# Fourth pair's values cast head by head on two engines, and a new hand-kept order for the first half, in an attention and MLP kernel

## The chip, the cores and the metric

The kernel runs on one core of one Trainium2 chip. The metric is the device time of one execution in microseconds. Seven executions of the kernel before were measured: 233.19 to 238.86 us, with a median of 233.5 us. One further execution was recorded by the hardware profiler; it took 235.44 us.

In the profile the engines have short names. PE is TensorE's matmuls and PEld its weight loads, DVE is VectorE, ACT is ScalarE, POOL is GpSimd, and SP is SyncE, which here only issues DMA transfers.

## What is computed

The inputs are queries, keys and values of shape (4 batches, 8 heads, 768 positions, 64). Heads 0, 2 and 6 are "retrieval" heads, with full causal attention. The other five are "streaming" heads: a query sees the first four positions (the sinks) and the 64 latest ones. The attention output, as 3072 tokens of 512 channels, goes through a two-layer MLP with a PReLU between the layers.

```python
scores = scale * np.matmul(q, k.transpose(0, 1, 3, 2))
stream_keep = causal & (is_sink | in_win)
scores = np.where(mask, scores, -1e9)
a = softmax(scores)
x = np.matmul(a, v)                      # to (3072, 512)
h = x @ w_in                             # 512 -> 2048
g = np.maximum(h, 0.0) + alpha * np.minimum(h, 0.0)
out = g @ w_out                          # 2048 -> 512
```

## The kernel before, in words

The work of attention is cut into 16 "pairs" of heads, numbered n = 0 to 15: four pairs for each batch, with heads (2, 6), (1, 5), (0, 4) and (3, 7) in turn. Pair 3 is the fourth pair of batch 0, heads 3 and 7, both streaming. The MLP is cut into eight token blocks t = 0 to 7, two for each batch, of 512 and 256 tokens. Block 0 can begin only when all four pairs of batch 0 are done.

Each piece of work is an "item" with a short name, and the string ORDER (line 14) lists all items. The items are emitted in exactly that order. Each engine runs its own instructions in the order in which they were emitted, so ORDER alone decides what stands behind what on each of the five engines and on each DMA queue. The names that matter here:

- Lq, Lk, Lv n: loads of queries, keys and values of a pair (`load_q`, `load_k`, `load_rows`, lines 204 to 249). They are issued by SyncE and share one hardware DMA queue, in order. A retrieval head's values are one transfer; a streaming head's are two, the second a tail of 24 rows.
- Cq, Ck, Cv n: casts from float32 to bfloat16. The engine is picked by the strings CQ, CK and CV (lines 301 to 303). `cast_v` (line 346) casts both heads of a pair in one instruction, on GpSimd for n below 6, and then calls `sinks` (line 306), which on GpSimd copies the four sink rows of each streaming head into the other six slots.
- Tq, Tk n: transposes of queries and keys on TensorE (`to_array`, line 355), and tq, tk n: the copies of the result out of PSUM.
- S n.h.m: scores on TensorE; s n.h.m: the exponential on ScalarE; m n.h.m: the mask on VectorE from pair 4 on.
- A n.h: the product with the values (line 554), a n.h: the division by the sum on VectorE, X n and x n: the transpose of the result into the MLP's input and its copy.
- P t.f: the first MLP layer for block t and column group f, with p (relu of the negative part on ScalarE) and g (PReLU on VectorE); O t.s: the second layer, with o (copy and store).
- wi0 to wi7 and wo0 to wo3: loads of w_in and w_out, issued by GpSimd on its own software DMA queue, with a cast on the way. wi0 and wi1 serve column groups 0 to 3, wi2 and wi3 groups 4 to 7, wi4 and wi5 groups 8 to 11, wi6 and wi7 groups 12 to 15.
- id, nms, nmr, kz, qz, vz, kfz, warm and others: constants, zero fills and idle matmuls that warm TensorE.

PSUM has eight banks. An item takes the bank that was given back longest ago in ORDER (`take`, line 145), so it can wait for the reader of an older item.

Scores of pairs 4 and later are collected (`one_score`, `emit_burst`, lines 409 to 430) until an item comes up that can't stand beside them. If both heads of the collection have at least 576 columns, the matmuls of the two heads are interleaved on the two halves of TensorE's rows (line 428); if not, they run one after the other (line 421).

Of the kernel before, what the change touches and what calls it, by code (L numbers as in the profile page):

```python
# [11 lines left out]


ORDER = """
Lq0.0 kz3 id zero Lk0 warm0 Ck0.1 qz0 Lk2 La Ck2.0 Lq0.1 vz3 nmr Cq0.0 Cq0.1 vz1 kz0 Lq1 Tq0.0 warm1 Lq2 kz2 Ck0.0
Ck2.1 qz Tk0.0 sz1 sz2 vz0 tq0.0 Cq1 Lk1 warm2 tk0.0 Tk0.1 Lv0 Ck1.0 Cq2 vo S0.0.0 s0.0.0 kz1 tk0.1 Ck1.1 S0.0.2
m6.0.2 Cv0 Tq0.1 m14.0.2 s0.0.2 Lk3 vz2 Tk2 S0.0.1 Lv1 tq0.1 Lq3 Tq1 s0.0.1 tq1 nms Lq5 Ck3.0 S0.1.1 tk2.1 Ck3.1
S0.1.2 Tk1 sz0 s0.1.1 tk2.0 Tq2 S0.1.0 A0.0 Cv1 tk1.0 s0.1.2 S1.0.0 s0.1.0 A0.1 S1.0.1 tq2 s1.0.0 s1.0.1 Lv2 Tk3 wi1
S2.1.1 wi0 so s2.1.1 tk1.1 wi2 S2.1.0 Lk4 a0.0 S1.1.1 s1.1.1 a0.1 X0 Cq3 A1.0 Cv2 Lv3 a1.0 Ck4.1 Lk5 s2.1.0 Cq5 S2.0.2
wi3 Lq4 s2.0.2 S1.1.0 s1.1.0 ro Lk6 Tq3 x0 tq3 S2.0.0 wi6 A1.1 S2.0.1 s2.0.0 wi7 A2.1 tk3.0 s2.0.1 a1.1 Ck4.0 nz1 Cv3  # L20
tk3.1 S3.0.0 S3.0.1 wi5 s3.0.1 s3.0.0 A2.0 a2.1 Tq5 Ck5.0 a2.0 Tk4 S3.1.1 kfz2 Lq6 s3.1.1 wi4 X1 x1 tq5 S3.1.0 X2
s3.1.0 idf x2 A3.0 tk4.0 tk4.1 Lk7 a3.0 P0.2.0 A3.1 P0.1.0 Al P0.1.1 P0.3.0 P0.2.1 a3.1 X3 Ck5.1 P0.3.1 x3 al Lv7 Lv4
P0.0.0 P1.0 P0.2.2 p0.2 P1.4 P0.1.2 p1.4 Cq4 P1.6 P0.3.2 g0.2 P0.0.1 Tk5 p0.1 p0.3 g1.4 g0.1 p1.6 tk5.0 g1.6 kfz3
P0.0.2 p0.0 g0.3 wo0 g0.0 P0.5.0 P1.2 tk5.1 P0.6 p0.6 p1.0 Tq4 P0.13 P0.5.1 P0.4.0 p1.2 g0.6 nz0 p0.13 P0.4.1 wo1 tq4
g1.0 P0.14 g1.2 P0.5.2 g0.13 P1.8 Ck6.1 p0.5 P0.10 Cq6 p1.8 p0.14 P0.4.2 g0.5 Lk8 p0.4 Tq6 Ck6.0 kfz0 tq6 P0.9 Lq7
P0.11 wo3 g1.8 p0.9 g0.14 kfz1 mr p0.10 wo2 g0.4 g0.9 S4.1.3 S4.0.0 S5.0.0 g0.10 S4.1.4 s4.1.3 P0.7 P0.8 s4.0.0 P1.14
p0.11 s4.1.4 p0.8 s5.0.0 Lv5 Cv4 p1.14 S4.1.2 S4.0.4 g0.11 s4.1.2 g0.8 ms P0.15 S4.1.1 s4.0.4 S5.1.2 p0.15 S5.0.2
S4.0.5 g1.14 s5.1.2 P0.12 g0.15 O0.0.0 p0.7 p0.12 P1.10 s4.1.1 s4.0.5 s5.0.2 g0.7 m4.0.5 m5.1.2 Lq8 Cv5 P1.12 S5.1.0
S4.0.3 S4.1.0 S4.0.1 g0.12 s4.0.3 O0.3.0 one m5.0.0 m4.0.0 O0.1.0 m4.1.4 Ck7.1 O0.0.1 O0.0.2 ns s5.1.0 p1.10 s4.1.0
S4.0.2 s4.0.1 m4.0.4 g1.10 m4.0.1 S5.1.1 S4.1.5 m4.0.3 S5.0.1 s5.1.1 m4.1.1 Lk9 s4.1.5 O0.1.1 O0.0.3 Ck7.0 s5.0.1  # L30
m4.1.3 Tk6 m5.1.1 s4.0.2 p1.12 o0.0 Cv7 Ck8 Tk7 A4.0 Cq7 m4.1.5 g1.12 Lv6 m5.1.0 tk6.1 O0.3.1 m5.0.1 Tq7 O0.3.2 m4.0.2
Lq9 tk6.0 tk7.0 Cq8 S6.0.1 S6.0.0 m5.0.2 tq7 A5.1 nr Dk8.1 a5.1 O0.1.2 a4.0 A5.0 O0.1.3 s6.0.1 tk7.1 m4.1.0 o0.1
S6.1.0 S6.1.2 S6.0.2 S6.0.4 a5.0 s6.1.2 Dq8 O0.3.3 m6.1.2 S7.1.2 s6.0.4 s6.0.0 s6.1.0 Dk8.0 O0.2.0 s6.0.2 S7.1.0 o0.3
S6.0.3 S6.0.5 S7.1.1 S6.1.1 Ck9 s7.1.0 O0.2.1 s7.1.2 O0.2.2 Cv6 m6.0.0 s7.1.1 X5 m7.1.0 A4.1 s6.1.1 S8.1.1 x5 s6.0.5
S7.0.2 s6.0.3 m6.0.5 S8.1.5 m6.0.4 S7.0.0 S8.1.4 S7.0.1 m6.0.1 m6.1.1 Dk9.0 m7.1.1 s7.0.1 m6.0.3 s7.0.0 Lv9 O0.2.3
A6.0 Cq9 m7.1.2 s8.1.1 s8.1.5 O1.1.0 a6.0 a4.1 s8.1.4 Dq9 O1.1.1 s7.0.2 m6.1.0 m7.0.0 A7.1 S8.0.0 S8.1.2 S8.1.0 S8.0.1
A6.1 s8.0.0 m7.0.1 m7.0.2 m8.1.1 O1.1.2 s8.0.1 Dk9.1 a6.1 X4 A7.0 a7.0 s8.1.0 X6 a7.1 O1.0.0 O1.0.1 O1.1.3 x6 Lv8 X7
S8.0.3 S9.0.1 Lq10 s8.1.2 Lq11 s9.0.1 Cv9 near1 S9.1.1 x7 O1.0.2 m8.1.0 o0.2 s8.0.3 O1.0.3 S9.1.2 S8.1.3 m8.1.4 S8.0.4
S9.0.2 o1.1 S9.1.0 m8.1.5 S9.0.0 s9.1.1 s8.1.3 s8.0.4 P2.6 Cv8 p2.6 Lk11 o1.0 m8.1.3 Lk10 P2.5 p2.5 P2.14 s9.1.2 P3.0
s9.1.0 s9.0.2 p2.14 P2.3 P2.7 Lq12 g2.6 Lq13 m9.1.0 p2.3 g2.5 s9.0.0 near0 m10.0.2 near2 A8.1 p3.0 g2.14 g2.3 g3.0  # L40
Cq11 p2.7 m9.1.1 m8.0.4 P2.0 p2.0 g2.7 P2.8 Lk12 g2.0 P2.2 p2.8 m9.1.2 S8.0.5 P2.13 p2.2 A9.1 Lk13 m8.0.1 g2.2 s8.0.5
m9.0.0 P3.14 P2.15 p2.13 g2.8 Ck11 P3.8 p2.15 P2.9 a8.1 g2.15 P3.4 P2.1 a9.1 P3.10 Ck10 p3.4 Dk10.0 g2.13 P2.11 p2.1
p3.10 g3.4 S8.0.2 P2.4 s8.0.2 p2.4 g2.1 P2.10 Cq10 Dk10.1 g3.10 p2.9 Dq10 m8.0.5 m8.0.0 P2.12 m8.0.3 P3.6 g2.9 Dk11.1
g2.4 p2.10 A8.0 O2.0.0 g2.10 O2.0.1 p2.11 p3.8 g2.11 Ck12 S10.0.1 S10.0.4 s10.0.1 g3.8 p3.14 O2.0.2 s10.0.4 Dk11.0
O2.1.0 Dq11 p2.12 a8.0 g3.14 S10.1.1 S10.0.0 p3.6 g2.12 m10.0.4 S10.1.0 S10.0.5 s10.1.0 s10.1.1 O2.1.1 Lv11 Cq12
O2.0.3 g3.6 S10.0.3 S11.0.0 m10.1.0 s10.0.5 s10.0.0 S11.1.2 S11.1.0 m9.0.2 S10.1.2 S10.0.2 s10.0.3 Cq13 O2.1.2 m10.0.0
s10.1.2 Lv10 Ck13 m9.0.1 m10.1.2 s11.1.2 m11.1.2 s11.1.0 Dk12.0 P3.2 s10.0.2 p3.2 A9.0 s11.0.0 O2.2.0 Dq12 S11.0.2
S11.1.1 m10.0.5 O2.1.3 S11.0.1 m10.0.3 Cv11 m11.0.0 m10.1.1 Dk13.1 m11.1.0 X8 m10.0.1 s11.1.1 Cv10 P3.12 p3.12 m11.1.1
a9.0 s11.0.1 O2.2.1 g3.2 A10.1 Dk13.0 o2.1 Dk12.1 g3.12 a10.1 Dq13 A10.0 A11.1 O2.2.2 m11.0.1 X9 o2.0 O2.3.0 O2.2.3
S12.1.5 S12.0.4 S12.0.2 a10.0 s11.0.2 S12.1.2 m11.0.2 a11.1 S12.0.1 s12.1.5 A11.0 Lq14 a11.0 X11 O2.3.1 O3.1.0 s12.0.4  # L50
s12.0.2 m12.0.4 X10 S13.0.1 O3.1.1 s12.1.2 Lk15 s12.0.1 S12.0.3 S13.0.2 S13.1.2 s13.0.1 S13.1.1 o2.2 S12.0.0 S12.1.0
s12.1.0 s12.0.0 Lk14 s12.0.3 s13.1.2 O2.3.2 Lv12 O2.3.3 m12.0.3 o2.3 O3.0.0 s13.1.1 s13.0.2 O3.1.2 S12.0.5 S13.1.0
S13.0.0 S12.1.4 P4.0 m12.0.1 P4.1 m13.1.2 Cq14 s13.1.0 s13.0.0 m12.1.0 P4.11 m12.0.0 p4.0 s12.0.5 P4.12 m13.1.0 P4.3
p4.1 g4.0 P4.4 m13.0.1 s12.1.4 p4.12 g4.1 Lq15 P5.6 p4.11 m12.0.5 p4.3 g4.11 O3.0.1 m13.1.1 g4.12 Ck15 g4.3 p4.4 P4.15
P4.13 P4.9 p4.13 Lv13 P5.2 p4.15 Ck14 Dq14 m12.0.2 Cv12 g4.4 g4.13 Dk15.1 P4.10 Cq15 g4.15 p5.6 g5.6 p4.10 P4.6 Cv13
Dk14.0 p4.6 g4.10 g4.6 A12.0 p5.2 O3.0.2 A13.1 O3.0.3 g5.2 a13.1 O3.1.3 P4.7 o3.0 S12.1.1 S14.0.3 P4.14 o3.1 P4.2
Dk14.1 p4.7 p4.9 Dq15 s12.1.1 a12.0 g4.7 g4.9 S15.1.2 S14.0.2 p4.14 S14.0.4 S15.1.1 S14.1.0 s14.0.3 m12.1.4 m12.1.1
p4.2 s14.0.2 P5.12 g4.14 m14.0.3 s14.1.0 P4.5 p5.12 g4.2 P4.8 s15.1.2 m13.0.2 O4.3.0 m13.0.0 Lv15 Dk15.0 s14.0.4 p4.5
S14.0.5 S15.1.0 S14.0.1 s15.1.1 S14.1.2 g5.12 g4.5 m15.1.1 p4.8 S12.1.3 g4.8 S14.0.0 s12.1.3 O4.3.1 A13.0 m12.1.3
s14.0.0 P5.14 Lv14 Cv15 S15.0.2 s14.0.5 s14.1.2 p5.14 S15.0.0 a13.0 m14.1.2 O4.3.2 S15.0.1 S14.1.1 m12.1.5 m15.1.2  # L60
s15.1.0 m14.0.5 Cv14 m15.1.0 s15.0.2 s15.0.0 A12.1 P5.8 A15.1 s14.0.1 m14.1.0 s14.1.1 P5.0 m14.0.1 m14.1.1 A14.1
m14.0.4 s15.0.1 a12.1 m14.0.0 O4.1.0 g5.14 a14.1 X13 A14.0 m15.0.0 P5.4 p5.8 m15.0.1 X12 m15.0.2 a15.1 A15.0 p5.0
a15.0 p5.4 O4.1.1 g5.8 O4.0.0 a14.0 m4.1.2 O4.2.0 g5.4 X15 P5.10 O4.1.2 O4.0.1 O4.2.1 m8.0.2 x15 X14 O4.0.2 P6.8 P6.6
O4.0.3 p5.10 g5.0 P6.1 O4.3.3 O4.2.2 g5.10 P6.7 p6.8 o4.0 p6.7 p6.6 P7.6 g6.7 g6.8 O4.2.3 P6.10 O4.1.3 P6.3 p6.10 o4.3
g6.10 P7.4 o4.2 O5.1.0 O5.1.1 P7.0 p6.1 g6.6 P6.2 g6.1 p6.3 O5.0.0 g6.3 o4.1 P6.13 p6.13 P7.14 g6.13 O5.0.1 p6.2 p7.0
P6.0 g6.2 O5.1.2 P6.5 g7.0 P6.11 p6.0 g6.0 O5.0.2 p6.11 O5.1.3 p7.4 p6.5 g6.11 P7.10 p7.14 m8.1.2 o5.1 g6.5 m12.1.2
P6.9 P6.4 g7.4 p6.9 g6.9 p6.4 O5.0.3 g7.14 P7.2 O6.1.0 P6.15 g6.4 p7.2 P7.12 p6.15 O6.1.1 O6.1.2 g7.2 o5.0 O6.0.0
g6.15 P6.14 P6.12 O6.0.1 p6.14 O7.0.0 O6.0.2 g6.14 p7.6 p7.12 p6.12 g6.12 g7.6 O6.3.0 O6.2.0 O6.2.1 O6.0.3 P7.8 O6.2.2
O6.1.3 g7.12 O6.3.1 p7.8 o6.1 p7.10 O6.3.2 O6.3.3 g7.8 O7.0.1 o6.3 g7.10 o6.0 L0 O6.2.3 O7.0.2 o6.2 O7.0.3 L1 l0 L2
o7.0 l1 l2  # L70
""".split()


@with_exitstack
def kernel(
    ctx: ExitStack,
    tc: tile.TileContext,
    q: bass.AP,
    k: bass.AP,
    v: bass.AP,  # L80
    is_retrieval: bass.AP,
# [7 lines left out]
    nc = tc.nc  # L89
    B, H, S, D = q.shape  # L90
# [9 lines left out]
    NSINK = 4  # L100
# [96 lines left out]
    def heads(n):  # L197
        return PAIRS[n % 4]
# [104 lines left out]
    CV = "PPPPPPVVVVVVVVVV"  # L303
    natq, natk, held = {}, {}, {}

    def sinks(n, rows):

        for hh, h in enumerate(heads(n) if n < LAY else ()):
            if not RETR[h]:
                vh = rows[0:NSINK, hh, :, 0:D].bitcast(fp32)  # L310
                nc.gpsimd.tensor_copy(vh[:, 1:7, :], vh[:, 0:1, :].to_broadcast([NSINK, 6, D // 2]))

    def part_of(buf, hh):
        return buf.rearrange("p a b d -> p (a b d)")[:, 6 * D * hh:6 * D * (hh + 1)]
# [27 lines left out]
        nt = 6 if RETR[heads(n)[hh]] else 7  # L342
        nc.sync.dma_start(kTs[n % NK][hh][:, 0:128 * nt].rearrange("p (i r) -> p i r", r=128),
                          natk[n][:, 896 * hh:896 * hh + 128 * nt], transpose=True)

    def cast_v(n):
        vv = vb[n % NV]
# [416 lines left out]
            item(f"Cq{n}", cast_q, n)  # L764
        item(f"Lk{n}", load_k, n)
        item(f"Lv{n}", load_v, n)
        item(f"Cv{n}", cast_v, n)
        if n < CROSS:
            for hh in range(2):
                item(f"Ck{n}.{hh}", cast_k, n, hh)  # L770
# [87 lines left out]
```

## Time and profile before

| what | value |
|---|---|
| median of seven runs | 233.5 us (233.19 to 238.86) |
| the profiled execution | 235.44 us |
| its span, first to last instruction | 233.7 us |
| TensorE busy | 221.6 us, 95% of the span |
| VectorE, ScalarE, GpSimd busy | 153.4, 138.9, 48.3 us |
| moved by DMA | 36.63 MB, 157 GB/s in the mean |
| granted TensorE clock | 1.00 |
| chain that ended last, by engine | PE 81%, DVE 8%, DMA 4% |

The page gives busy time by engine, a row of 40 slices of the span for each engine (each digit is tenths of a slice, 9 is 90% or more), the chain of work that ended last, and groups of instructions by line. Further views give busy time in chosen stretches (windows), the instructions of one engine in order of time (timeline), and who waited for whom. In a timeline a line has the start, the duration, the engine, the line of the program, the operation with its tiles, and in brackets the idle time ahead of it with what ended it. A busy TensorE is not TensorE at its peak, since the ends of matmuls are modelled. The idle time of an engine that is not the bound costs nothing.

### The profile page before, as it was taken

The page shows a single profiled execution, that of the slowest core. Times are in us where ns is not written, and L with a number is a line of the kernel's source. Part 1 is how long each engine was busy: PE and PEld are TensorE (multiplying, and loading weights), DVE is VectorE, ACT ScalarE, POOL GpSimd, SP SyncE. Part 2 cuts the span into 40 slices and gives each one's busy share as a digit, 9 for nine tenths or more (in the row PEclk, how much of TensorE's full clock was granted, in tenths as well). Part 3 has the DMA queues.
Part 4 walks back from the last instruction along what each step waited for, and adds up shares of the span by engine and source line. Part 5 has one row for each costly group of instructions (what it writes and reads, how often), then busy time and mean ns, then how long its engine had stood idle before and what let it go on. Part 6 is the DMA issues. An engine that isn't in the chain of part 4 may idle for free.

```text
span 233.7 us, 5202 instructions
## 1 busy us (share of the span) xinstructions
PE 221.6 (95%) x1970; PEld 136.5 (58%) x1998; DVE 153.4 (66%) x393; ACT 138.9 (59%) x280; POOL 48.3 (21%) x97
## 2 busy tenths in 40 slices
PE   6989769999999999999999999999999999999994
PEld 5778747555465665566466545655864555554553
DVE  4696646898796855998998267979990245545110
ACT  5578546998699539837764874498522333623231
POOL 3778768001294004000001000010000020000000
PEclk9999999999999999999999999999999999999999
DMA  5989999999999899948999999895310130110033
GB/s 187 307 231 207 229 240 248 206 195 194 240 196 206 170 206 254 247 86 158 194 152 143 259 241 188 158 175 97 72 34 0 45 137 1 45 46 1 0 135 136
DMA packets 92449, 36.63 MB, mean 157 GB/s; under 512 B 79472, under 2 KB 90632, under 8 KB 92424
## 3 DMA queue, kind: packets, MB, share of 16 engines
q1 hardware_dynamic: 86168, 26.97, 56.6%
q0 software_dynamic: 5792, 8.93, 18.4%
q10 hardware_dynamic: 464, 0.40, 0.6%
q8 instruction: 15, 0.25, 0.4%
q14 instruction: 10, 0.08, 0.1%
HBM read 27.55 MB, written 6.29 MB: 145 GB/s over the span
## 4 chain that ended last, share of the span: by engine, by line
PE 81%; DVE 8%; DMA 4%; issue 2%; SPq 1%; POOL 1%; ACT 1%; POOLq 0%; ACTq 0%; DVEq 0%
PE P L619 33%; PE P L599 33%; PE P L554 6%; DMA vf<-in_v_dram 4%; PE P L428 3%; DVE g L611 2%; PE P L421 2%; PE P L702 2%; PE P L638 2%; DVE kT L390 1%; DVE kT L386 1%; DVE xn L565 1%; PE P L579 1%; PE P L361 1%; DVE eR L477 1%
## 5 line engine op out<-in xcount | busy, mean ns | idle before, releaser
L611 DVE SCALAR_TENSOR_TENSOR g<-neg,oma,P 128x512 bf16<-128x512 f32 (+1 forms) x128 | 72.9, 609 | 38.5 <-ACT neg L604 37.3
L599 PE MATMUL P<-xT,w_in_b 128*128 128x256 bf16 (+1 forms) x503 | 89.3, 325 | 0.4
L604 ACT ACTIVATE neg<-P 128x512 f32<-128x512 f32 x96 | 54.8, 605 | 54.0 <-PE P L599 46.5
L619 PE MATMUL P<-w_out_b,g 128*128 128x512 bf16 x349 | 84.7, 379 | 1.4 <-issue 0.5
L599 PEld LDWEIGHTS <-w_in_b 128*128 128x128 bf16 x512 | 48.9, 98 | 32.2 <-issue 0.2
L619 PEld LDWEIGHTS <-g 128*128 128x128 bf16 x368 | 34.1, 98 | 36.2 <-issue 1.6
L467 ACT ACTIVATE eR<-P 128x448 bf16<-128x448 f32 (+6 forms) x63 | 36.0, 620 | 12.8 <-PE P L460 3.5
L629 POOL DMA_DIRECT2D out_dram<-ot x18 | 9.9, 550 | 126.8 <-ACT ot L625 126.6
L565 DVE TENSOR_TENSOR xn<-P,rcp 128x448 bf16<-128x448 f32 (+1 forms) x32 | 19.4, 608 | 1.1
L625 ACT COPY ot<-P 128x512 f32<-128x512 f32 x23 | 13.3, 595 | 9.1 <-PE P L619 6.7
L521 ACT ACTIVATE eS<-P 128x384 bf16<-128x384 f32 (+1 forms) x25 | 13.3, 569 | 6.3 <-PE P L499 3.2
L515 ACT ACTIVATE eS<-P 128x352 bf16<-128x352 f32 x30 | 13.7, 484 | 5.3 <-PE P L421 4.8
L554 PE MATMUL P<-vb,eS 128*128 128x65 bf16 x260 | 11.3, 193 | 1.8 <-POOL vb L348 1.5
L554 PEld LDWEIGHTS <-eS 128*128 128x128 bf16 x260 | 10.2, 97 | 4.7 <-issue 2.1
L411 PE MATMUL P<-qT,kT 128*128 128x192 bf16 (+13 forms) x68 | 11.2, 250 | 0.9 <-DVE qT L368 0.8
L564 DVE RECIPROCAL rcp<-P 128x7 f32<-128x7 f32 (+1 forms) x32 | 6.3, 198 | 8.0 <-PE P L554 7.8
L530 DVE TENSOR_TENSOR eS<-eS,ms_near 128x352 bf16<-128x352 bf16 x30 | 9.5, 334 | 2.6 <-ACT eS L515 2.4
L348 POOL CAST vb<-vf 128x896 bf16<-128x896 f32 x6 | 5.6, 940 | 25.1 <-DMA vf<-in_v_dram 25.1
L477 DVE TENSOR_TENSOR eR<-eR,mr_near 128x128 bf16<-128x128 bf16 (+5 forms) x36 | 6.9, 224 | 5.1 <-ACT eR L467 5.1
L554 PE MATMUL P<-vb,eR 128*128 128x65 bf16 x276 | 10.3, 192 | 0.0
L428 PE MATMUL P<-qT,kT 64*128 64x176 bf16 (+13 forms) x159 | 10.2, 251 | 0.0
L554 PEld LDWEIGHTS <-eR 128*128 128x128 bf16 x276 | 9.6, 97 | 1.0
(100 smaller groups left out, 187.1 us busy)
## 6 DMA issues: line engine op xcount, KB each, us to landing
out_dram<-ot POOLq DMA_DIRECT2D x18, 256.0 KB, 4.2
vf<-in_v_dram SPq DMA_DIRECT2D x22, 192.0 KB
kf<-in_k_dram SPq DMA_DIRECT2D x21, 192.0 KB
qf<-in_q_dram SPq DMA_DIRECT2D x18, 192.0 KB
qf<-in_q_dram SPq DMA_DIRECT2D x7, 384.0 KB
w_in_b<-in_moe_w_in_dram POOLq DMA_DIRECT2D x8, 256.0 KB, 8.6
w_out_b<-in_moe_w_out_dram POOLq DMA_DIRECT2D x4, 512.0 KB, 12.8
kf<-in_k_dram SPq DMA_DIRECT2D x9, 196.0 KB
```

What stands on the lines that cost most here:

```text
L411: nc.tensor.matmul(to, keys, queries, start=True, stop=stop)
L428: nc.tensor.matmul(to, keys[own], queries[own], start=True, stop=True)
L467: nc.scalar.activation(ebuf[n, hh][:, lo:hi].rearrange("p (x c) -> p x c", x=len(parts)), P[:, got[0]:got[0] + len(parts), 0:(hi - lo) // ...
L515: nc.scalar.activation(slots, sc[:, 0:352].rearrange("p (s c) -> p s c", c=176), AF.Exp, scale=scale)
L521: nc.scalar.activation(slots, sc.rearrange("p x (s c) -> p x s c", c=192), AF.Exp, scale=scale)
L554: nc.tensor.matmul(pav[:, i, :], e[:, o:o + 128], vv[:, j, hh, 0:D + 1], start=(m == 0), stop=(m == len(terms) - 1))
L565: nc.vector.tensor_tensor(xn[n][:, 0:nt, D * hh:D * hh + D], pav[:, :, 0:D], rcp.to_broadcast([128, nt, D]), op=ALU.mult)
L599: nc.tensor.matmul(psg[:, w * i:w * (i + 1)], w_in_b[:, c, 128 * fb:128 * (fb + 1)], xT[:, c, o:o + w], start=(x == 0), stop=(x == 3))
L604: nc.scalar.activation(neg[t, f], bank(held["P", t, f][0]), AF.Relu, scale=-1.0)
L611: nc.vector.scalar_tensor_tensor(g_buf[t % 2][:, fb, 0:w], neg[t, f][:, c], oma[:, fb:fb + 1], bank(got[0])[:, c], op0=ALU.mult, op1=ALU.add)
L619: nc.tensor.matmul(bank(held["O", t, s][0]), g_buf[t % 2][:, f, 128 * s:128 * (s + 1)], w_out_b[:, f, :], start=(f == 0), stop=(f == 15))
L625: nc.scalar.copy(ot, bank(got[0]))
```

## The change

The item Cv3 becomes two items, Cv3.0 and Cv3.1. The first casts head 3 on GpSimd and copies its sink rows there, the second does the same for head 7 on VectorE. The other pairs are cast as before.

```diff
-    def sinks(n, rows):
-
-        for hh, h in enumerate(heads(n) if n < LAY else ()):
-            if not RETR[h]:
+    def sinks(n, rows, of=range(2), copy=nc.gpsimd.tensor_copy):
+
+        for hh in of if n < LAY else ():
+            if not RETR[heads(n)[hh]]:
                 vh = rows[0:NSINK, hh, :, 0:D].bitcast(fp32)
-                nc.gpsimd.tensor_copy(vh[:, 1:7, :], vh[:, 0:1, :].to_broadcast([NSINK, 6, D // 2]))
+                copy(vh[:, 1:7, :], vh[:, 0:1, :].to_broadcast([NSINK, 6, D // 2]))
...
+    def cast_v_head(n, hh):
+        vv = vb[n % NV]
+        cast_of("PV"[hh])(vv[:, :, hh, 0:D], vf[n % NF][:, :, hh, :])
+        sinks(n, vv.rearrange("p t h c -> p h t c"), [hh], (nc.gpsimd.tensor_copy, nc.vector.tensor_copy)[hh])
...
-        item(f"Cv{n}", cast_v, n)
+        if n == 3:
+            for hh in range(2):
+                item(f"Cv{n}.{hh}", cast_v_head, n, hh)
+        else:
+            item(f"Cv{n}", cast_v, n)
```

ORDER is new from its beginning up to about the item p2.13, and the same behind it. What each engine gets, in its order, around the places that the text speaks of:

```
GpSimd before: kz3 id Ck0.1 ... Cv1 wi1 wi0 wi2 Cq3 Cv2 Ck4.1 Cq5 wi3 wi6 wi7 Ck4.0 nz1 Cv3 wi5 Ck5.0 kfz2 wi4 Ck5.1 Cq4
GpSimd after:  id nmr kz3 nms Ck0.1 ... Cv1 wi1 Cq3 Cv2 wi0 wi2 Ck4.1 Cq5 Cv3.0 wi3 wi7 Ck4.0 wi6 kfz0 Ck5.1 Ck5.0 wi5 Cq4 wi4

TensorE before: S3.0.0 S3.0.1 A2.0 Tq5 Tk4 S3.1.1 X1 S3.1.0 X2 A3.0 P0.2.0 A3.1 P0.1.0 Al P0.1.1 P0.3.0 P0.2.1 X3
TensorE after:  S3.1.0 A2.0 S3.0.1 Tq5 S3.1.1 X2 X1 S3.0.0 A3.1 Tk4 A3.0 P0.3.0 P0.3.1 Al P0.1.0 P0.1.1 X3

VectorE before: a2.1 a2.0 x1 x2 idf a3.0 a3.1 x3 al
VectorE after:  a2.1 a2.0 Cv3.1 x1 x2 idf a3.1 a3.0 x3 al

ScalarE before: s3.0.1 s3.0.0 s3.1.1 tq5 s3.1.0 tk4.0 tk4.1 p0.2 p1.4 p0.1 p0.3
ScalarE after:  s3.1.0 s3.0.1 s3.1.1 s3.0.0 tk4.0 p0.1 tq5 p0.2 p1.0 tk4.1 p0.3

Loads (SyncE) before: Lq0.0 Lk0 Lk2 Lq0.1 Lq1 Lq2 Lk1 Lv0 Lk3 Lv1 Lq3 Lq5 Lv2 Lk4 Lv3 Lk5 Lq4 Lk6 Lq6 Lk7 Lv7 Lv4 Lk8 Lq7 Lv5 Lq8 Lk9 Lv6 Lq9
Loads (SyncE) after:  Lq0.0 Lq0.1 Lk0 Lq1 Lk1 Lq2 Lk2 Lv0 Lk3 Lv1 Lq3 Lv2 Lq5 Lk4 Lv3 Lk5 Lq4 Lq6 Lk7 Lq8 Lv5 Lk6 Lq7 Lk8 Lv4 Lv6 Lq9 Lk9
```

The built program has the same number of TensorE instructions as before. Of the 204 score matmuls of the pairs from 4 on, 45 were emitted alone and 159 interleaved before; after, 34 are alone and 170 interleaved.

## The prediction

> **What bounds the kernel now.** I read the page first (busy shares, the 40 slices), then the stages by window, then TensorE's timeline and GpSimd's around the idle places, and the chain of waits in order of time.
>
> ```profile
> PE 221.6 (95%) x1970; PEld 136.5 (58%) x1998; DVE 153.4 (66%) x393; ACT 138.9 (59%) x280; POOL 48.3 (21%) x97
> PE   6989769999999999999999999999999999999994
> PEclk9999999999999999999999999999999999999999
> DMA  5989999999999899948999999895310130110033
> ```
>
> TensorE is full from the eighth slice on, at the full granted clock; only the first six or seven slices (up to about 36 us) have holes. DMA is full over the same 36 us and nearly so up to 100 us.
>
> ```profile
> 12.00:24.00 12.00, 11.01 (x189) 9.68 (x189) 9.48 (x26) 9.79 (x15) 8.97 (x19) 1.00 1.00 220
> 24.00:30.00 6.00, 4.63 (x81) 4.19 (x80) 3.41 (x10) 3.36 (x6) 4.31 (x7) 1.00 1.25 220
> 30.00:36.00 6.00, 4.41 (x49) 2.81 (x50) 2.67 (x7) 1.83 (x3) 5.00 (x11) 1.00 1.17 262
> 36.00:48.00 12.00, 11.90 (x86) 7.71 (x87) 9.49 (x20) 10.65 (x23) 3.92 (x7) 1.00 1.21 217
> ```
>
> The first number behind the comma is TensorE's busy time. It lacks 1.4 us in 24 to 30, 1.6 us in 30 to 36, and 0.1 us in the next 12. ScalarE has 10.65 of 12 us in that last window, so the first MLP phase is nearly full on ScalarE too. TensorE's timeline names the two holes:
>
> ```profile
> 27.53 0.51 PE L363 MATMUL P<-ident,natm 128*128 128x128 bf16 x6 [1.19 <-POOL natm L333]
> ...
> 31.35 0.22 PE L554 MATMUL P<-vb,eS 128*128 128x65 bf16 x2 [1.53 <-POOL vb L348]
> 31.75 0.49 PE L554 MATMUL P<-vb,eS 128*128 128x65 bf16 x11 [0.18 <-POOL vb L311]
> ```
>
> The first is the transpose of pair 4's keys, behind GpSimd's cast; the second is pair 3's product with its values. GpSimd shows why both are late:
>
> ```profile
> 25.12 1.84 POOL L707 DMA_DIRECT2D w_in_b<-in_moe_w_in_dram  x3
> 26.93 0.55 POOL L333 CAST natm<-kf 128x384 bf16<-128x384 f32 x1
> ...
> 30.37 0.93 POOL L348 CAST vb<-vf 128x896 bf16<-128x896 f32 x1 [2.06 <-DMA vf<-in_v_dram]
> 31.36 0.63 POOL L311 COPY vb<-vb 4x192 f32<-4x192 f32 x2
> ```
>
> The key cast stood behind three w_in issues; the value cast waited for its load. The chain agrees:
>
> ```profile
> 20.44 9.78 DMA vf<-in_v_dram
> ...
> 30.37 0.94 POOL vb L348
> 31.36 0.35 POOL vb L311
> 31.75 0.51 PE P L554 x11
> ```
>
> So up to 33 us the values of pair 3 set the end; from there it is TensorE's own work. A microsecond won or lost before 33 us, or a hole behind it, is a microsecond of the kernel.
>
> **The change, step by step.** Its own time is 235.44 us, a span of 233.7 and 1.7 around it; the median of the runs is 233.5, 1.9 lower. I add up differences and set them against both.
>
> *Warm-up (a gain that is hidden).* The identity now comes before the 0.84 us key fill on GpSimd, so the first matmul moves from 2.22 to about 1.4, and the first key transpose and copies come 0.9 us earlier. ScalarE's chain of exponentials starts at about 8.2 instead of 9.01. In it the before lost some 4.9 us idle (1.99 at 28.47, 0.98 at 15.26 and smaller). The new TensorE order has the key transpose Tk4 and its wait behind all four scores of pair 3, so I get the last exponential at about 28 instead of 30.37. This costs nothing and alone brings nothing: the values are still out. If they came early, this cover would be what is late next.
>
> *Value load.* Ahead of pair 3's values the load queue has the same loads as before, in another order. By the trace's landing marks (16 per transfer, one a DMA engine) head 3 landed at a median of 24.8 but on the last engine at 28.82 (its tail 29.09), head 7 at 29.75 (tail 30.22). The last engine was the one with three w_in transfers in front (last marks 24.80, 26.60, 28.54). Two of the three now stand behind the cast of pair 2's values: issue at about 21.1 and 21.8 instead of 19.04 and 19.66. A w_in issue at 18.27 had its first packet at 20.68, 2.4 us later, so they reach the engines at 23.5 and 24.2, when the first w_in transfer is only just done there (24.80 on the last). The backlog does not break. [...] Bounds for this step: -2.5 us (the backlog breaks, values run as fast as the load queue alone did at 18 us, 1043 packets of 256 B in one us) to 0. I take 0: landing at 28.8 for head 3, 29.8 for head 7.
>
> *Cast by head.* Head 3 no longer waits for head 7 (1.1 us), and its cast is a 128x448 one: between the rows of 0.50 (384) and 0.94 (896), 0.58; one 4x192 copy, 0.31, of the two that take 0.63. With 0.15 to be released GpSimd is done 1.1 us after landing, 29.9. Head 7 on VectorE: the 128x384 cast there is 0.35, so some 0.4; the 4x192 copy has no row on VectorE, between its 64x20 copy (0.17) and GpSimd's 0.31, I take 0.25. Done at 30.5. Behind it on VectorE wait the two copies x1 and x2 (0.56 each), done at 31.6, just ahead of the MLP.
>
> *What is late next.* GpSimd now issues two w_in transfers (0.62 each) and only then casts head 2 of pair 4's keys (0.52): 29.9 + 1.24 + 0.52 = 31.7. TensorE does A3.1 at 30.5, then Tk4 waits for that cast, 31.7 to 32.1, and A3.0 behind it takes 0.6: the MLP begins at about 32.7. By TensorE's own work up to there (starts to next starts, long waits cut off) the before had 25.61 us done at 32.88, and the after will have 25.36 at 32.7. The lead is 7.34 against 7.27 us of lost time, and 7.56 against about 7.5 once X3 is in. So the start is worth 0.0 us, within half a us.
>
> *Idle TensorE.* All of pair 3's scores are in at about 27.6; until A3.1 TensorE stands 2.9 us. [...] The trace has 1.53 us as its longest late hole and a granted clock of 1.00 in every window. [...]
>
> *Score bursts.* Scores of batches 1 and up run two at a time on TensorE's halves when enough of both lie together (L428), else alone (L421). The built order moves 11 matmuls of 204 from alone to paired: 45 and 159 become 34 and 170. By columns of pairs 4 to 9: alone 4236 become 1703, the longer halves of the paired 9006 become 10401; 1138 columns less. At 216 ns for 512 columns (L599: 0.86 for 4) this is -0.48 us, straight on the bound. Burst counts stay at nine, so their fill and drain stays.
>
> *ScalarE and VectorE in the first MLP phase.* tq5 (0.79) and tk4.1 (0.81) move into it. ScalarE then has 24 relus at 0.5 from start to start and 6.2 us of copies, 18.2 us from 35.3 on, against TensorE's 22 from 32.7 on: done before it. Banks: at most 8 in use, full for a moment at 42.5. Between 0 and +1; I take 0. w_in 3, 7, 6, 5, 4 follow from 29.9 to 35 instead of 25 to 33.8 and land some 1 us later than they did, 3 us or more ahead of use; w_out lands by about 55, wanted at 57.
>
> *Loads behind.* The load queue now takes pair 7's keys, queries 8 and values 5 ahead of keys 6, queries 7 and keys 8. Counted below as the rival.
>
> Sum: 0.0 - 0.5 + 0.1 for X3 waiting on its copies = -0.4. Own time 235.0, median 233.1.
>
> **Rivals.**
>
> *The backlog breaks* (gain). If the two later w_in transfers leave a gap of half a us, the remaining thousand or so value packets pass in little over 1 us. Head 3 lands at 26, and TensorE's order is bound by the exponentials at about 28 and by Tk4's cast at 29: the MLP starts 2 us earlier. 233.1 - 2.1 = 231.0. For it: two transfers moved by 2.2 us. Against: the last engine's marks above.
>
> *Keys 6 arrive late* (slower). Keys 6 now stand behind 3120 packets of 256 B (queries 8, values 5). From 42 to 52 us the load queue moved 144 packets a us beside w_out, alone 860. So: some 650 by 42, 1760 more by 54.2, the rest by 55.0, keys 6 at about 56.1. VectorE wants them (Ck6.1) at about 56.4, where before they lay ready from 38.8. VectorE is a strict queue: behind it stand the masks m5.x and m4.x, for which A5.1 waits on TensorE at 60.8. 3 us of VectorE work lies between, so it decides from a landing of about 57.5 on, one for one; at 59.5, which is reached if w_out ends 3 us later than before, +2, and keys 8 (wanted right behind) another 0.3: 233.1 + 2.3 = 235.4.
>
> [...]
>
> **How the numbers follow.** Start unchanged, bursts cheaper: 0.37, 233.1 (232.4 to 233.9). Backlog breaks: 0.25, 231.0 (230.5 to 232.2). Keys late: 0.30, 235.4 (233.9 to 236). Clock: 0.08, 234.8. A measurement here tells about 0.2% (0.47 us) from no change. Faster by more: 0.25 and 0.15 of the first case, 0.40. Same: 0.20 of the first. Slower: the other two and a rest, 0.40. Range 231.0 to 235.3: it leaves out some 0.1 at each end.
>
> **What would show it.** Right: GpSimd's 128x448 cast at 28.9 to 29.2 released by the load, key cast Tk4 waits on at about 31.3, MLP start (first L599) at 32.5 to 33, 34 matmuls on the alone line. Backlog broken: the cast before 27. Keys late: a VectorE wait of over 1 us for kf near 56 and a TensorE hole near 60. Wrong altogether: new holes of TensorE between 36 and 55, that is a relu or bank wait I counted at nothing.

## The result, and the profile after

Over 26 runs the changed kernel has a median of 231.78 us (231.18 to 234.74). The kernel before, in all 61 of its runs, has 234.94 (232.03 to 242.04); the seven runs shown ahead of the prediction had 233.5. The ratio is 0.9924, with a 95% interval of 0.9907 to 0.9941: 0.8% faster, some 1.8 us. The forecast of 233.1 was 1.3 us too high; the rival *the backlog breaks* had said 231.0. As gains over the kernel before, the forecast was 0.4 us, the rival's 2.5, and the ratio gives 1.8. Runs with a lower mean granted clock are longer (of the kernel before's that the experiments took along, the 25 at 0.993 or less have a median of 238.05 us, those at 0.997 or more 234.2), and the ratios leave most of them out.

The profiled execution took 231.55 us, its span 229.8, against 235.44 and 233.7. That is 3.9 us, twice the difference of the runs, because the execution of before that was profiled lies 1.2 us above the median, 234.2, of the kernel before's runs at a clock of 0.997 or more that were taken along with the experiments. The page's head:

```profile
PE 220.7 (96%) x1970; PEld 136.1 (59%) x1998; DVE 151.9 (66%) x395; ACT 139.5 (61%) x280; POOL 47.3 (21%) x96
PE   7989879999999999999999999999999999999994
PEclk9999999999999999999999999999999999999999
```

The fifth and sixth slices, up to some 34 us, now read 8 and 7, where they read 7 and 6; behind them TensorE is full as before. The same stages by window:

```profile
12.00:24.00 12.00, 11.22 (x205) 10.07 (x203) 9.60 (x26) 9.70 (x14) 9.46 (x16) 1.00 1.03 241
24.00:30.00 6.00, 4.18 (x83) 3.99 (x81) 4.43 (x11) 2.97 (x5) 4.27 (x10) 1.00 1.17 264
30.00:36.00 6.00, 6.00 (x41) 3.64 (x41) 2.47 (x6) 2.98 (x5) 5.47 (x9) 1.00 1.20 219
36.00:48.00 12.00, 11.89 (x81) 7.19 (x82) 10.08 (x21) 11.56 (x25) 0.00 (x0) 1.00 1.21 197
```

The first 12 us after, and then before:

```profile
0.00:12.00 12.00, 10.04 (x114) 8.37 (x115) 8.83 (x24) 8.36 (x9) 8.16 (x22) 1.00 0.92 256
```

```profile
0.00:12.00 12.00, 9.00 (x99) 7.72 (x100) 6.79 (x19) 7.16 (x8) 6.41 (x16) 1.00 0.87 246
```

TensorE's busy time, the first number behind the comma of each row, sums to 31.44 us from 0 to 36 us; before it was 29.05. So 2.4 us of the 3.9 are more work done by 36 us, 1.0 of it already by 12. From 36 to 48 nothing changed (11.89 against 11.90), though ScalarE is now busy for 11.56 of the 12. Another 0.9 us is less TensorE work in all (220.7 against 221.6), and the remaining 0.6 is idle time behind 36 us. GpSimd shows what moved:

```profile
20.72 1.24 POOL L712 DMA_DIRECT2D w_in_b<-in_moe_w_in_dram  x2
...
23.16 0.57 POOL L348 CAST vb<-vf 128x448 bf16<-128x448 f32 x1
23.79 0.34 POOL L311 COPY vb<-vb 4x192 f32<-4x192 f32 x1
...
25.29 0.52 POOL L333 CAST natm<-kf 128x384 bf16<-128x384 f32 x1
```

Head 3's cast is at 23.16, with no wait, where I had 28.9 to 29.2; the prediction had set 27 as the mark below which the backlog has broken. By the landing marks head 3 was in at 22.39 (its tail at 22.62) against 28.82, head 7 at 25.62 (25.95) against 29.75. TensorE behind it:

```profile
27.41 0.55 PE L559 MATMUL P<-vb,eS 128*128 128x65 bf16 x13 [0.54 <-DVE xT L589]
27.80 0.50 PE L368 MATMUL P<-ident,natm 128*128 128x128 bf16 x6
28.13 0.55 PE L559 MATMUL P<-vb,eS 128*128 128x65 bf16 x13
29.97 0.59 PE L604 MATMUL P<-xT,w_in_b 128*128 128x512 bf16 x2 [1.28 <-DMA qf<-in_q_dram]
```

The values are hardly waited for any more: the 0.54 us is for a copy on VectorE, behind the second half of the cast. The MLP starts at 29.97 (its first matmul before was at 32.09), behind a new wait of 1.28 us. The profile names queries as its end, but wi0, the second w_in transfer, had its last mark at 29.61, and the weight load that goes ahead of these matmuls starts 0.11 us behind it:

```profile
29.72 0.34 PEld L604 LDWEIGHTS <-w_in_b 128*128 128x128 bf16 x3 [1.16 <-issue]
```

So the wait is for wi0; the first and fifth experiments agree.

### The profile page after: what moved, and what is told of

It is laid out like the page before. It is cut to its first block, busy times and chain, and to the rows that moved or that the text cites. A ratio compares the mean times of both kernels' runs of the same rounds, so it can differ in the third digit from the quotient of the medians.

```text
span 229.8 us, 5202 instructions
## 1 busy us (share of the span) xinstructions
PE 220.7 (96%) x1970; PEld 136.1 (59%) x1998; DVE 151.9 (66%) x395; ACT 139.5 (61%) x280; POOL 47.3 (21%) x96
## 4 chain that ended last, share of the span: by engine, by line
PE 80%; DMA 7%; ACT 4%; SPq 3%; issue 2%; POOL 2%; ACTq 0%; POOLq 0%
PE P L604 35%; PE P L624 32%; PE P L559 5%; DMA qf<-in_q_dram 4%; PE P L433 4%; DMA kf<-in_k_dram 2%; SPq L247 2%; PE P L643 2%; DMA vf<-in_v_dram 1%; SPq L224 1%; PE P L426 1%; ACT kT L395 1%; PE P L584 1%; POOL vb L353 1%; ACT eR L472 1%
## 5 line engine op out<-in xcount | busy, mean ns | idle before, releaser
L416 PE MATMUL P<-qT,kT 128*128 128x192 bf16 (+14 forms) x68 | 11.3, 250 | 1.1 <-ACT qT L373 0.7
L433 PE MATMUL P<-qT,kT 64*128 64x176 bf16 (+17 forms) x170 | 10.8, 251 | 0.0
L433 PEld LDWEIGHTS <-kT 64*128 64x128 bf16 x170 | 6.7, 94 | 5.9 <-issue 5.1
```

Source lines behind the costliest of these rows:

```text
L416: nc.tensor.matmul(to, keys, queries, start=True, stop=stop)
L433: nc.tensor.matmul(to, keys[own], queries[own], start=True, stop=True)
```

## The experiments

Theory at the start: the time is made before 33 us, by pair 3's values landing 4 us earlier, because two w_in transfers no longer stand beside them. Rivals: the load queue's own new order did it, the cast by head did it, or the paired scores did.

**The start alone.** The order of the change up to X3, that of before behind it.

```
 ORDER after: id Lq0.0 warm0 ... A3.1 Tk4 A3.0 idf P0.3.0 ... X3
+ORDER before, from there on, what is not yet emitted: Lv7 P0.0.0 P1.0 ...
```

> The changed kernel's order up to X3 (with its split cast), and behind it the order of the kernel before, so 45 score matmuls alone as before. Theory V (the gain is made before 33 us, by pair 3's values landing some 4 us earlier): about 2.3 us of the lead stays, the first-layer start at 30 to 31 us as in the changed kernel, median 232.2 to 232.5. Theory B (the gain is the paired scores, the start only shifts where TensorE waits): nearly all is lost, about 233.4.

Measured: median 232.51 (231.7 to 238.46), ratio to before 0.9921 (0.9885 to 0.9956). By the ratio all of the gain is the start's, by the medians all but 0.7 us. TensorE reaches the MLP at 30.13, and here the profile gives the wait in the same place its right name:

```profile
30.13 0.81 PE L603 MATMUL P<-xT,w_in_b 128*128 128x512 bf16 x3 [1.02 <-DMA w_in_b<-in_moe_w_in_dram]
```

Its span is 231.0, 1.2 over the changed kernel's; its last matmuls start 0.8 us later, of which 0.2 to 0.4 stem from the start itself (30.13 for 29.97, and 31.03 for 30.65 at the next group).

**Only w_in later, in the kernel before.**

```
-... wi1 wi0 ... wi2 ... Cq3 ... Cv2 ... Ck4.1 Cq5 wi3
+... wi1 ... Cq3 ... Cv2 wi0 wi2 ... Ck4.1 Cq5 wi3
```

> The kernel before with wi0 and wi2 moved behind Cv2, nothing else. Theory W (the values were held up by the burst of w_in issues; moving them frees the load queue): last mark of head 7 at 27 us or earlier against 29.75, the cast at 28 or earlier, median 1.5 us below the kernel before. Theory L (what counts is that the load queue gets the value packets in before wi1 starts at 20.7 us, through Lv2 standing ahead of Lq5 and an earlier start): head 7 stays near 29, median within 0.4 us of the kernel before. My recorded prediction said 0 for this move.

Measured: head 3 landed at 24.36, head 7 at 25.83, against 28.82 and 29.75. Theory W holds for the landing, by this one move (which also let the values be issued 0.8 us earlier, at 18.23). But the median is 234.31 and the ratio 0.9988 (0.9943 to 1.0033): no gain that can be told, though the interval leaves room for 1.3 us, and in the trace pair 3's last transpose, X3, is 0.9 us earlier than before (33.54 for 34.47). The trace shows what took the rest. GpSimd came to the cast only behind three w_in issues, a key cast and a zero fill:

```profile
24.64 1.84 POOL L706 DMA_DIRECT2D w_in_b<-in_moe_w_in_dram  x3
26.44 0.55 POOL L332 CAST natm<-kf 128x384 bf16<-128x384 f32 x1
26.88 0.95 POOL L292 MEMSET natk<- 128x960 f32 x1
27.72 0.97 POOL L347 CAST vb<-vf 128x896 bf16<-128x896 f32 x1
```

The cast no longer waits for its data, it waits in its queue. And on TensorE the moved transfer itself is now late; wi0's last mark is 31.02. It was issued only at 22.20, since the cast Cv2 ahead of it waited 1.30 us for pair 2's values; in the changed kernel the load queue takes these values earlier, Cv2 waits for nothing, and wi0 is out at 20.72. This speaks for the two moves belonging together:

```profile
20.91 0.94 POOL L347 CAST vb<-vf 128x896 bf16<-128x896 f32 x1 [1.30 <-DMA vf<-in_v_dram]
```

```profile
31.15 0.59 PE L598 MATMUL P<-xT,w_in_b 128*128 128x512 bf16 x2 [1.43 <-DMA w_in_b<-in_moe_w_in_dram]
```

**w_in back, in the changed kernel.**

```
-... wi1 ... Cq3 ... Cv2 wi0 ... wi2
+... wi1 ... wi0 wi2 Cq3 ... Cv2
```

> The changed kernel with wi0 and wi2 put back ahead of Cq3, directly behind wi1. Theory W: the values of pair 3 are late again (head 7 at 29 us or later) and 1.5 to 2 us are lost, about 233.5. Theory L: the values still land before 27 us because they pass ahead of wi1; w_in itself comes earlier, so the wait of the first MLP matmul for it (1.28 us at 29.97) goes; but GpSimd's casts Cq3 and Cv2 come 1.2 us later; about 231.5 to 232.

Measured: 230.63 to 236.6 in six runs: two at a granted clock of 1.00 took 230.63 and 230.74, four at 0.985 to 0.993 took 234.97 to 236.6. The ratio, from the two alone, is 0.983 (0.9719 to 0.9941), so what this move costs is seen in the four only. The profiled one is of the four. There head 3 is in at 23.57, as Theory L says, and head 7's last mark is 29.57 again, as Theory W says; in the two short runs the values probably came early, which no trace shows. What makes the long ones that long is in TensorE's rows:

```profile
31.10 0.73 PE L558 MATMUL P<-vb,eS 128*128 128x65 bf16 x13 [3.29 <-DVE xT L588]
...
32.26 0.92 PE L558 MATMUL P<-vb,eS 128*128 128x65 bf16 x13
```

```profile
28.00:31.00 3.00, 0.00 (x0) 0.00 (x0) 1.09 (x4) 0.66 (x1) 0.00 (x0) 1.00 1.14 296
31.00:34.00 3.00, 2.90 (x35) 2.17 (x34) 2.17 (x7) 0.79 (x1) 1.31 (x3) 0.55 1.18 234
34.00:38.00 4.00, 4.00 (x28) 2.36 (x27) 1.12 (x4) 1.03 (x2) 2.43 (x5) 0.91 1.10 211
```

TensorE stood for 3.29 us, and then 13 matmuls took 0.92 us in place of 0.55. The third number from the end is the granted clock: 0.55.

How the transfers pass each other is best seen in the packets. Per us from the stated time on, the load queue's packets of 256 bytes (values) and those of w_in:

```
from us            20   21   22   23   24   25   26
before: values      0    0   27  469  234  130  252
        w_in        6   96   94   86  153  159  135
after:  values    694  152  392  207  139    0    0
        w_in       10  138   78   25   76   94   95
w_in later: values 175  434  207  710   51    7    0
        w_in        0  107  137   12    0    1  152
w_in back: values   3  541  304  279  185   95   72
        w_in        0    3  111   89  149  144  145
```

Beside w_in at full flow (130 and more of its packets in one us) the values pass at between half and twice its number (252 to 135, 152 to 138, 72 to 145); in a gap of w_in they pass at 700 in one us. One transfer is 256 packets (107, 137 and 12 in the third pair of rows). In the changed kernel the values found two gaps: ahead of the first w_in packet, and up to 24 us, as the first transfer ran out (10 + 138 + 78 + 25 = 251). Before, 282 had moved by 24 us: the second transfer followed without a pause.

**One cast for both heads, in the changed order.**

```
-Cv3.0                ... wi6 X1 Cv3.1
+                     ... wi6 X1 Cv3
```

> The changed kernel's order with one cast of pair 3's values for both heads on GpSimd, at the place where the VectorE half stood (behind wi6). Theory S (the cast head by head on two engines is worth something): the cast and its sink copies are done at about 28.1 us against 24.1 and 26.6 us, so A3.1 and Tk4 are 1 to 1.5 us later and 1 us or more is lost, 232.8 or more. Theory V (only the landing counts; behind it the first MLP matmul waits for w_in until 29.97 anyway): A3.1 at about 28.3 and A3.0 at 28.9 still lie ahead of 29.97, and the time stays within 0.3 us of the changed kernel, 231.5 to 232.1.

Measured: 231.97 (231.23 to 232.97), ratio 0.9891 (0.9822 to 0.9961). Theory V: the cast by head, which gives the change its name, is worth nothing that can be measured. The whole cast took 0.93 us at 25.86, and TensorE went on to the MLP at 28.72, since in this execution wi0 was in at 27.96. That start is 1.25 us ahead of the changed kernel's and the span is the same, 229.8; VectorE waited 1.1 us for the keys of pair 6. So between these two executions, what was won at the start was lost again behind it.

**wi0 one place earlier, in the changed kernel.**

```
-wi1 ... Cq3 ... Cv2 wi0 ... wi2
+wi1 ... Cq3 ... wi0 Cv2 ... wi2
```

> The changed kernel with wi0 one place earlier on GpSimd, between Cq3 and Cv2 (issue near 19.5 us in place of 20.72), wi2 kept. The changed kernel's first MLP matmul stood 1.28 us, until 29.97, and wi0's last mark was 29.61. Theory W2 (that wait is for w_in, and one w_in transfer in front of the values does no harm): wi0 lands by about 28.5, the wait shrinks to 0.3 us, 0.7 to 1 us gained, 230.8 to 231.1. Theory Q (the wait is for the queries that the profile names, or the earlier w_in holds up the values): 231.8 or more, with head 7 landing after 27 us in the second case.

Measured: median 232.39 of 12 runs, the lowest 230.53, 235 and more in four (one of them 290.17, at a clock of 0.757); ratio 0.9903 (0.9857 to 0.9949). The eight at a clock of 1.00 have a median of 231.3, so a small gain of this move is neither shown nor excluded. In the profiled run (span 230.6) wi0 landed at 27.56 and the MLP began at 29.06 with no wait named, so Theory W2 is right on the cause. In this run the 0.9 us won there was lost again, and 0.8 more: between 44 and 70 us TensorE waited 1.2 us for w_out and VectorE 1.1 us for the keys of pair 6.

**The cast by head alone, in the order of before.**

```
-nz1 Cv3 tk3.1
+nz1 Cv3.0 Cv3.1 tk3.1
```

> The kernel before, with pair 3's values cast head by head on GpSimd and VectorE where the one cast stood; no other order is changed. Theory S (the split is worth what it takes off the value path): head 3's cast starts at its own landing, near 29, head 7's on VectorE near 30.3, so the MLP starts up to 0.8 us earlier: 0.3% below the kernel before. Theory V (only the landing of the values counts, and behind it GpSimd's other work): within 0.2% of the kernel before, and the long runs of 237 us and more, at a granted clock below 1, are still there.

Measured: 240.27 (238.68 to 242.1), ratio 1.0282 (1.0211 to 1.0354). Both theories missed it. VectorE is a strict queue, and tk3.1, the copy of pair 3's keys, stands behind the new cast, which waited 7.02 us:

```profile
31.32 0.42 DVE L347 CAST vb<-vf 128x448 bf16<-128x448 f32 x1 [7.02 <-DMA vf<-in_v_dram]
...
32.05 0.94 DVE L394 COPY kT<-P 64x744 bf16<-64x744 bf16 x1
```

TensorE stood 6.24 us for that copy, and its granted clock was 0.70 from 28 to 31 us and 0.50 from 31 to 34. So the edit to the cast, without its place in the new order, costs 6 us, the fallen clock included.

**Only the load order, in the kernel before.**

```
-Lq5 ... Lv2
+Lv2 Lq5
```

> The kernel before with the load of pair 2's values ahead of pair 5's queries, nothing else. Theory L (the load queue's own order brought the values in earlier): Cv2 and, through it, the w_in issues move, head 7 lands at 28 us or earlier, and 0.5 us or more is gained. Theory W (only the number of w_in transfers ahead of the values counts, and it is still three): head 7 at 29.5 or later, within 0.3% of the kernel before.

Measured: median 236.38 (231.55 to 239.59), ratio 0.9948 (0.9888 to 1.0009): unclear. Head 3 landed at 22.55, 6.3 us earlier, so Theory L has its share; head 7, whose packets met all three w_in transfers, landed at 28.65. TensorE still waited 1.8 us for the values' cast, and behind that wait the granted clock of this run was 0.51 from 31 to 34 us (last section). The load order brings the first head in, moving w_in the second.

**Idle matmuls in the hole.** Sixteen, then thirty-six, ahead of A3.1 in the kernel with w_in back.

```diff
-    for i, n in enumerate((28, 3, 14)):
+    for i, n in enumerate((28, 3, 14, 16)):
-... S3.0.0 kfz0 s3.1.1 x1 A3.1
+... S3.0.0 kfz0 s3.1.1 x1 warm3 A3.1
```

> The kernel of the third run (changed kernel, wi0 and wi2 back ahead of Cq3) with 16 idle matmuls of 128 columns ahead of A3.1, some 0.9 us of work that computes nothing. In the third run TensorE stood 3.29 us there, the granted clock in the next 3 us was 0.55, and four of its six runs took 235.0 to 236.6 us at a mean clock of 0.985 to 0.993, the other two 230.6 and 230.7. [...]

> The kernel of the eighth run with 36 idle matmuls in place of 16 (2.4 us at the 66 ns apiece of that run; they compute nothing). With 16, TensorE still stood 2.90 us when the values were late, and the granted clock fell to 0.68 some 1.2 us later. Theory G (the idle stretch sets the clock): with a stretch of about 1.6 us, as the kernel before had at a clock of 1.00, the clock stays at 1.00 in all runs, and none is longer than 235; the short runs rise to 232 or more, since the values are there before the idle matmuls end. Theory N: runs of 236 to 239 us at a mean clock below 0.995 remain.

Measured with 16: 235.96 (232.85 to 238.85), and the clock still fell, to 0.68 from 31 to 34 us, behind a hole of 2.90. With 36: 233.42 (232.34 to 235.16), all 12 runs at a clock of 0.998 or more. In its profiled run the values were late too (head 7 at 29.03):

```profile
26.81 2.17 PE L706 MATMUL P<-ident 128*128 128x128 bf16 x36
30.58 0.55 PE L558 MATMUL P<-vb,eS 128*128 128x65 bf16 x13 [1.59 <-DVE xT L588]
```

The product behind the hole takes 0.55 us for its 13 matmuls, where the third run's second product took 0.92. Theory G of the run with 36 holds in this: with the idle stretch filled to 1.59 us the clock was 1.00 from 28 to 38 us. With 16, six of the 12 runs were at 0.993 or less, with 36 none; 20 more matmuls that compute nothing took 2.5 us off the median of all runs, and 0.7 off that of the runs at 0.997 or more (234.1 to 233.4). In the load-order run the clock fell behind a hole of 1.80 us, not much longer; the last section has the rows.

**Pair 5's queries later**, alone and with wi0 earlier.

```
-Lq5 Lk4 ... Lv3      Cq5 Cv3.0 ... Ck4.0       Tq5 S3.1.1 ... A3.0
+Lk4 ... Lv3 Lq5      Cv3.0 ... Ck4.0 Cq5       S3.1.1 ... A3.0 Tq5
```

> The changed kernel with the load of pair 5's queries (Lq5) behind pair 3's values instead of ahead of pair 4's keys, its cast (Cq5) behind Ck4.0 and its transpose (Tq5) behind A3.0, in TensorE's hole ahead of the MLP. Theory W (the values compete with what shares the DMA engines in front of them): one load less in front brings head 7 in 0.5 us or more earlier, and the transpose fills 0.3 us of the wait for w_in; the wait for w_in (wi0 lands near 29.6) stays: 231.2 to 231.8, with a spread no wider than the changed kernel's. Theory P (the wait for w_in is the bound of the start, nothing ahead of it counts): 231.6 to 232.

> Both moves: pair 5's queries behind pair 3's values as in the ninth run, and wi0 between Cq3 and Cv2 as in the fifth, whose short runs took 230.5 to 231 us and whose long ones 233 to 237. Theory W: with one load less ahead, the values are in before the earlier w_in transfer can hold them up, so the long runs go and the median is 230.5 to 231.0, the best of all. Theory D (behind the start the loads of keys 6 and of w_out are the next bound: the fifth run waited 1.1 and 1.2 us for them): 231.5 or more in spite of an MLP start before 29.2 us, with a VectorE wait for kf or a TensorE wait for w_out of 1 us.

Measured: 232.46 (231.04 to 234.63), ratio 0.9896 (0.9855 to 0.9936); and 232.13 (231.26 to 233.71), 0.9905 (0.9858 to 0.9952). Neither is shown to be better than the change. The loads did what was asked (head 7 at 22.43 in the first; the MLP at 28.68 in the second), and Theory D took it back: the second then waited for the cast of pair 4's queries (0.97 us at 35.88), w_out (1.6) and on VectorE the keys of pair 6 (1.6).

**Two bursts alone.**

```diff
-        if min(columns) < SPLIT:
+        if min(columns) < (840 if burst and burst[0][0] < 6 else SPLIT):
```

> The changed kernel with two of its bursts of pairs 4 and 5 (18 score matmuls, 832 and 832 columns in the shorter halves) emitted alone instead of interleaved: 1664 columns more on TensorE, at 216 ns for 512 columns 0.70 us. Theory C (TensorE is full there, each column counts): 0.6 to 0.9 us lost, 232.4 to 232.7, and the recorded step of -0.48 us for 1138 columns is of the right size. Theory E (the exponentials or masks behind the scores set the pace, so pairing is worth little): less than 0.3 us lost, 231.8 to 232.1; then the 0.7 us that the first run lost against the changed kernel came from elsewhere in the order.

Measured: 232.33 (230.75 to 234.48, six runs), ratio 0.9875 (0.9802 to 0.9948), so the runs show no loss. The two profiled executions, which both start the MLP's matmuls at 30.0 us within 0.05, are easier to compare: pair 5's product A5.1 begins at 60.55 against 60.25, and the span is 230.1 against 229.8. That is 0.3 us for 1664 columns, not 0.70, as far as one execution of each can tell: each theory is half right.

**Taken together.** The gain is in the order up to X3 (first run). The cast by head has no measurable part in it, and the paired scores, by the last run, some 0.2 us. Within the start, neither of the two moves that bring the values in shows a gain alone. How the gain divides among the early values, wi0's early issue and the earlier first 12 us is not shown: no run takes one of these from the changed kernel and keeps the others.

## Why the prediction was wrong in its likeliest case

The measured median lies inside my range of 231.0 to 235.3, but at the end that a rival had put there. My likeliest case, a start worth 0.0 us, did not come, and that the range holds the result is due to the rival (0.25), not to the sum. The rival in turn was right that the backlog breaks; what it held to bind next, the exponentials and Tk4's cast, was not what did, so that its 2.5 us came near the measured 1.8 is in part luck.

**Value load: the step that failed.** I took 0 for moving wi0 and wi2 behind Cv2 ("The backlog does not break"), with 28.8 and 29.8 as landings. Measured: 22.39 and 25.62, and 25.83 for head 7 by this move alone. My working followed the last DMA engine, where the first w_in transfer would just be done when the moved ones came, and found no gap. But the transfer issued at 20.72 moved its packets only from about 24.2 us on, when the first had run out, and that pause was enough. I had taken 2.4 us from an issue to its first packet; in the changed kernel it was 3.0 for the first transfer (17.88 to 20.84) and some 3.5 for this one. In addition the new load order, which I had counted as nothing for this step, brought the issue of the values forward from 19.00 to 17.34 (17.22 with that order alone), so that 694 packets were through in one us ahead of nearly all of w_in. I had set bounds of -2.5 to 0 and took the end that fitted one engine's marks; 2.4 us is what TensorE gained by 36 us.

How the two queues share an engine, no run shows by itself. By count the packets were not far from even beside w_in at full flow, half to two value packets for each w_in packet; by time they were not. In the changed kernel's us from 21 on, the records of 138 w_in packets sum to 1.03 us an engine in the mean of the 16, 120 ns a packet, and those of 152 value packets, 23 ns each, to 0.22 us. (Records overlap: the DMA share is 1.17 from 24 to 30 us.) The values moved fastest where w_in was nearly absent: 694 packets in the us from 20 on, beside 10 of w_in.

**What is late next.** I named Tk4's key cast at 31.7 and the MLP at 32.7. The cast was at 25.29. Late next was wi0, the moved transfer itself, at 29.61, with the MLP at 29.97. I had asked what w_in did to the values, and whether the later transfers met their use, but not whether wi0, first in use, still came in time.

**Warm-up.** "Hidden, brings nothing" was true only with late values. With early ones it counts: TensorE had done 1.0 us more by 12 us and kept it to 36 us, since it now waits only 0.54 us on the values' path. That this is a part of the gain is argued, not shown; the second experiment, with early values and the old warm-up, has none that can be told.

**Cast by head.** The durations were right but for one (0.57 for 0.58, 0.34 for 0.31; on VectorE 0.56 for 0.4, and 0.25 for 0.25), but the split is worth nothing here (231.97 without it). What I didn't see is what the VectorE half costs in the wrong place.

**Idle TensorE.** My sum has no time for the 2.9 us of idle. The change never met it (0.54 and 1.28, clock 1.00). Where it was met, at 2.90 with the sixteen idle matmuls, the clock was 0.68 from 31 to 34 us: had the values been as late as I forecast, the changed kernel might have paid for it. The clock fell behind 1.80 us too (0.51 in the load-order run), and not behind 1.53 in the kernel before or 1.59 with thirty-six (1.00). The clock case of the forecast, 234.8, counts 1.7 us for a drop, a term that no run shows; in the third experiment the two runs at a clock of 1.00 took 230.63 and 230.74, the four at 0.985 to 0.993 took 234.97 to 236.6, some 4.2 to 6.0 us more, and in the profiled one of these the values were late as well.

**Score bursts.** -0.48 for 1138 columns at full price. The nearest measurement, 0.3 for 1664, makes it an estimated -0.2; the start-only kernel gives up to 0.5 us for all of the later order. Right in sign, at most half in size.

**ScalarE and VectorE in the first MLP phase.** 0, and the window from 36 to 48 us shows 11.89 against 11.90.

**Keys 6.** The rival did not come, by little. I had them at 56.1 and wanted at 56.4; their last mark was 56.25 and VectorE came to them at 56.48, with no wait. The kernels that start sooner than the change do wait, 1.1 to 1.6 us.

What stays open: why a few of the sixteen landing marks come 1 to 2 us behind the others (of head 7's, twelve came by 24.06 and four between 24.87 and 25.62), and what sets whether w_in leaves a gap. Both may be part of the spread of the runs, as the clock is.

## What to carry to other kernels

When two queues share the DMA engines, ask where the bulky one pauses: here the small urgent load passed in the pauses (694 packets in a us beside 10 of w_in, 152 in the next beside 138), and moving wi0's issue by 3.2 us (19.04 to 22.20, second experiment, with wi2 behind it and the values issued 0.8 us earlier) moved head 7's landing by 3.9 (29.75 to 25.83). Then put the moved transfer itself on the list of what is late next. A wait added to a strict queue costs what stands behind it, so a cast that is harmless in one order costs 6 us in another (here 6.24 us of TensorE, behind tk3.1). And at a start bound by loads, each us won soon meets the next load, here w_out and the keys of pair 6 (1.2 and 1.1 us in the fifth experiment).

## What the runs showed of the hardware

The mean granted TensorE clock of the profiled executions was 0.986 to 0.993 in the third, sixth, seventh and eighth experiments and 0.998 or more in all others. In the four the rows show the fall between 28 and 38 us, around the longest idle stretch that TensorE had on its way to the MLP. In each row TensorE's busy time is the first number behind the comma and the clock the third from the end. The third experiment's rows stand above (hole of 3.29 us; clock 0.55, then 0.91). The sixth, with a hole of 6.24:

```profile
28.00:31.00 3.00, 0.00 (x0) 0.10 (x1) 0.00 (x0) 0.00 (x0) 1.69 (x4) 0.70 1.25 231
31.00:34.00 3.00, 0.76 (x8) 0.75 (x8) 2.56 (x8) 0.00 (x0) 2.03 (x5) 0.50 1.18 258
34.00:38.00 4.00, 3.95 (x57) 3.68 (x56) 2.53 (x8) 2.64 (x4) 1.85 (x4) 0.74 1.19 241
```

The seventh (load order), with a hole of 1.80:

```profile
30.09 0.22 PE L553 MATMUL P<-vb,eS 128*128 128x65 bf16 x2 [1.80 <-POOL vb L347]
```

```profile
28.00:31.00 3.00, 1.02 (x19) 0.81 (x17) 0.56 (x1) 2.30 (x4) 1.82 (x4) 0.92 1.18 248
31.00:34.00 3.00, 2.78 (x23) 1.50 (x22) 1.66 (x4) 0.00 (x0) 1.54 (x5) 0.51 1.17 244
34.00:38.00 4.00, 4.00 (x33) 2.77 (x32) 0.94 (x3) 0.66 (x2) 3.56 (x6) 1.00 1.17 257
```

The eighth (sixteen idle matmuls), with a hole of 2.90:

```profile
28.00:31.00 3.00, 0.10 (x4) 0.07 (x3) 1.27 (x4) 0.00 (x0) 0.00 (x0) 1.00 1.14 287
31.00:34.00 3.00, 2.80 (x36) 1.60 (x37) 1.98 (x6) 0.79 (x1) 1.66 (x4) 0.68 1.19 236
34.00:38.00 4.00, 4.00 (x26) 2.52 (x25) 1.16 (x3) 1.15 (x2) 4.00 (x7) 0.81 1.12 200
```

With thirty-six idle matmuls and a hole of 1.59 it stayed up:

```profile
28.00:31.00 3.00, 1.41 (x32) 1.28 (x30) 1.62 (x5) 0.00 (x0) 1.64 (x5) 1.00 1.16 295
31.00:34.00 3.00, 2.95 (x39) 1.92 (x37) 1.93 (x6) 0.79 (x1) 2.19 (x4) 1.00 1.27 199
```

The fall came late with the sixteen idle matmuls: the product right behind the hole still took 0.55 us for its 13 matmuls at 30.92, as with thirty-six, and two w_in matmuls at 32.41 took 1.06 us, where with thirty-six they took 0.59 at 31.91. Of the holes named here the clock fell with those of 1.80 us and more, and stayed at 1.00 with 1.59 and, in the kernel before, 1.53. Whether the length of the hole is what decides, and what sets how long the clock stays low, these rows do not show.
